# A layernorm, S4 convolution and gated MLP on one core: the last four token tiles' convolution sums in two halves, and a new order of instructions

## The chip, the cores and the metric

The kernel runs on one core of a Trainium2 chip. A core has five engines with queues of their own: TensorE (PE, matrix products), VectorE (DVE), ScalarE (ACT), GpSimd (POOL) and SyncE (SP). Here SP and POOL issue most DMA transfers. The metric is the device time of one execution in microseconds (us), as the median of several runs; lower is better.

## What is computed

The sum of three terms over 2048 tokens of 512 channels: the input x, an S4 layer's long convolution of the normalized input (its kernel is made from 128 complex modes per channel, and it has a skip term), and a gated MLP of the normalized input with 1792 hidden features.

```python
def reference(A_u, A_A_re, A_A_im, A_B_re, A_B_im, A_C_re, A_C_im, A_log_dt, A_Dskip, B_x, B_w_gate, B_w_up, B_w_down):
    def _A_ref(u, A_re, A_im, B_re, B_im, C_re, C_im, log_dt, Dskip):
        ...
        P = jnp.exp(logdA[:, :, None] * l[None, None, :])
        K = jnp.einsum("dn,dnl,dn->dl", Cc, P, dB).real
        ...
        Yf = Uf * Kf[None, :, :, :]
        ...
        y = (lambda x, *d: x.transpose(*d))(y, 0, 2, 1) + u * Dskip[None, None, :]
        return y
    def _B_ref(x, w_gate, w_up, w_down):
        g = jnp.einsum("bsd,df->bsf", x, w_gate)
        u = jnp.einsum("bsd,df->bsf", x, w_up)
        h = _sigmoid(g) * u
        return jnp.einsum("bsf,fd->bsd", h, w_down)
    x = A_u
    xn = _layernorm(x, axis=-1)
    return x + _A_ref(xn, A_A_re, A_A_im, A_B_re, A_B_im, A_C_re, A_C_im, A_log_dt, A_Dskip) + _B_ref(xn, B_w_gate, B_w_up, B_w_down)
```

Kf and Uf are Fourier transforms over 4096 points of the convolution kernel K and of the normalized input.

## The kernel before

Tokens are 16 tiles of 128 rows, `acc` holds the result and starts as x, `xn` the normalized input. Channels go in two halves of 256 (b = 0, 1). The work is cut into some 880 steps; a step is what one call of `add` records, and it issues one or several instructions on one engine. Names of steps used below, with the lines at which they are issued:

- norm0 to norm15 (L467 on DVE, L471 on ACT): layernorm of a tile. xT loads transpose it for the MLP.
- Kernel of the convolution, for each half b: parameters (around L635/L637), then levels Ha, Hc, Hd, He (L658 to L661), which build powers of 64 in `H`, and levels G1 to G16 (L694, L695, L698), which build the low powers in `G` through `tB`. All of these are DVE's. kgen (L723) multiplies both on PE into PSUM `pk`; ke (L338 on ACT, L339 on DVE, as all plain evictions from PSUM) copies it to `ks`; dump transfers write it to `kt_scr` in DRAM; exp transfers load it, spread, to `kf`.
- dsk (L779): one short DVE instruction that adds the skip term into row 0 of `kf`. It waits for the first two exp transfers of its half.
- s1k (L815): PE's first stage of the kernel's transform, `kf` to PSUM `pzk`; zke evicts, zkw writes to `zk_scr` in DRAM, lk loads it in another layout. The input goes the same way: s1x (L796), zse, zw, `z_scr`, lx.
- For eight groups of frequencies per half: px and pk (L935, 64x64 forms on PE) make the second stage, xe evicts px to a buffer in `H` or `xn`, two sw transfers copy it within the chip with its parts exchanged, kx copies pk to the ring (ACT), xk (L947, DVE) multiplies, or does so straight from PSUM, and kx falls away; pv (L963, PE) goes back one stage, ve evicts, vw writes to `v_scr`.
- inv (L989, PE): the last stage, for four token tiles (m = 0 to 3) in two inv steps each, from vp loads of `v_scr`; yo (L994, DVE) adds PSUM `py` to `acc`.
- The MLP in eight pairs of tiles: g and u steps (L834, eight matmuls each, called gate/up groups here), sig (L867, ACT), then up on ACT (L872) and a product of two ring buffers on DVE (L871), or the product straight from PSUM on DVE and no copy on ACT; d…a and d…b (L844, eight and six matmuls) are the down projection; ge (L889, DVE) adds it to `acc` for tiles 12 and up (`LATE` = 12), for the others ACT evicts, or DVE adds.
- sb and st transfers store `acc`: sb for tiles 0 to 11, st12 for tiles 12 and 13, st14 and st15.

The order of instructions on every engine is a written list: `ORDER` has the numbers of all steps, `OTHER` those which run on their other engine (DVE for ACT, POOL for SP), `SLOT` which of the ring, pair and PSUM buffers each use takes. Waits follow from these. Four PSUM buffers are shared by everything on PE, and 18 ring buffers (and more, from `tmp`, `G`, `gm` and `tB` when these are free) by the loads and evictions. A step carries a cost, a `move` time and, for a transfer, a `pre` time. `emit` reads none of the three:

```python
    def emit(self):
        for n in OTHER:
            t = self.tasks[n]
            t.eng, t.cost, t.fn = t.alt
        slots = dict(zip([b.n for b in self.bufs if b.kind in ROOM], SLOT))
        for n in ORDER:
            t = self.tasks[n]
            ...
            t.fn()
```

## Time and profile before

| | us |
| --- | --- |
| median of three runs | 229.45 |
| lowest and highest | 228.29, 232.39 |
| the profiled execution | 230.61 |
| its span | 228.8 |
| ACT busy in the span | 168.2 |
| POOL busy in the span | 74.1 |

The granted clock of TensorE was 0.996 in the profiled execution. The span goes from the first to the last instruction of the profile, and the execution's time has 1.81 us around it. All numbers of the trace are places or durations in that span. An arrow in a row (out<-in) tells what an instruction writes and reads; a row that joins several instructions has their number behind an x.

### The profile page before, as it was taken

How to read it: one execution, taken by the hardware profiler on the slowest of the kernel's cores; microseconds unless marked ns; L12 is line 12 of the kernel's file. 1: busy time of each engine (PE TensorE's matmuls, PEld its weight loads, DVE VectorE, ACT ScalarE, POOL GpSimd, SP SyncE). 2: the span in 40 equal slices, each digit the busy share in tenths (PEclk: the TensorE clock that was granted, in tenths of full speed). 3: DMA queues.
4: the chain of work that ended last, by engine and by line, in shares of the span. 5: the costliest groups of instructions: out<-in, count | busy, mean ns of one | idle time of the engine just before them, and what ended most of it. 6: DMA issues, size and time to landing. Idle time of an engine off the chain costs nothing.

```text
span 228.8 us, 5263 instructions
## 1 busy us (share of the span) xinstructions
PE 207.9 (91%) x2073; PEld 140.9 (62%) x2088; DVE 195.2 (85%) x262; ACT 168.2 (73%) x208; POOL 74.1 (32%) x122
## 2 busy tenths in 40 slices
PE   7698699999989999999897999999699979999691
PEld 2377586568774549887575644777567856556240
DVE  1899999999999999999999999984877869942782
ACT  2499999999899999999997608787697554761100
POOL 1105705100013350760251241369345514043220
PEclk9999999999999999999999999999999999999998
DMA  5997597260832545469744897568967896877854
GB/s 161 243 338 256 145 305 278 57 198 34 229 95 30 218 142 150 78 174 261 260 181 161 247 257 196 146 186 225 295 243 276 228 352 199 278 227 227 320 150 141
DMA packets 50121, 46.84 MB, mean 205 GB/s; under 512 B 16912, under 2 KB 41072, under 8 KB 50096
## 3 DMA queue, kind: packets, MB, share of 16 engines
q1 hardware_dynamic: 42000, 26.07, 40.9%
q0 software_dynamic: 6592, 19.12, 26.2%
q10 hardware_dynamic: 1504, 1.31, 2.2%
q8 instruction: 16, 0.26, 0.5%
q14 instruction: 9, 0.07, 0.1%
HBM read 24.82 MB, written 15.37 MB: 176 GB/s over the span
## 4 chain that ended last, share of the span: by engine, by line
PE 31%; DVE 31%; ACT 16%; DMA 12%; issue 6%; SPq 1%; POOL 1%; another core or an unknown queue 0%; ACTq 0%; POOLq 0%; DVEq 0%
PE pg L834 9%; DVE tB L694 6%; DVE G L695 6%; PE pu L834 6%; PE po L844 5%; DVE G L698 4%; DMA tmp<-zk_scr 4%; DVE ring L871 3%; DMA ring<-v_scr 3%; PE pv L963 2%; ACT ring L338 2%; PE pk L723 2%; DMA out_dram<-acc 2%; DMA kf<-kt_scr 2%; ACT ring L867 2%
## 5 line engine op out<-in xcount | busy, mean ns | idle before, releaser
L834 PEld LDWEIGHTS <-W 128*128 128x128 bf16 x896 | 85.2, 98 | 22.1 <-issue 9.6
L834 PE MATMUL pg<-ring,W 128*128 128x256 bf16 x512 | 62.1, 273 | 0.1
L834 PE MATMUL pu<-ring,W 128*128 128x256 bf16 x384 | 48.1, 273 | 2.7 <-DVE tmp L339 1.3
L844 PE MATMUL po<-wd,ring 128*128 128x512 bf16 x176 | 43.5, 379 | 0.7 <-issue 0.3
L844 PEld LDWEIGHTS <-ring 128*128 128x128 bf16 x184 | 17.3, 98 | 20.5 <-issue 2.4
L867 ACT ACTIVATE ring<-pg 128x1024 bf16<-128x1024 f32 (+1 forms) x27 | 24.3, 900 | 3.3 <-PE pg L834 3.1
L698 DVE TENSOR_TENSOR G<-G,tB 128x256 bf16<-128x256 bf16 (+4 forms) x20 | 19.7, 986 | 0.7
L694 DVE TENSOR_TENSOR tB<-G,gm 128x256 bf16<-128x256 bf16 (+4 forms) x20 | 19.6, 981 | 0.5
L872 ACT ACTIVATE ring<-pu 128x1024 bf16<-128x1024 f32 x14 | 14.3, 1028 | 7.3 <-PE pu L834 7.3
L695 DVE TENSOR_TENSOR G<-G,gm 128x256 bf16<-128x256 bf16 (+4 forms) x20 | 19.6, 979 | 0.0
L338 ACT ACTIVATE ring<-pzx 128x1024 bf16<-128x1024 f32 x16 | 16.2, 1037 | 0.8 <-PE pzx L796 0.7
L994 DVE TENSOR_TENSOR acc<-py,acc 128x1024 bf16<-128x1024 f32 x8 | 9.5, 1220 | 5.6 <-PE py L989 5.5
L435 DVE BATCH_NORM_STATS2 stats<-acc 128x6 f32<-128x512 bf16 x16 | 9.9, 679 | 4.6 <-DMA acc<-in_A_u_dram 4.6
L324 POOL DMA_DIRECT2D z_scr<-ring x9 | 5.0, 553 | 26.6 <-ACT ring L338 26.6
L723 PE MATMUL pk<-H,G 128*128 128x84 bf16 x256 | 10.5, 199 | 2.6 <-DVE G L698 2.0
L871 DVE TENSOR_TENSOR ring<-ring 128x1024 bf16<-128x1024 bf16 (+1 forms) x17 | 10.3, 606 | 2.7 <-ACT ring L872 2.7
L723 PEld LDWEIGHTS <-G 128*128 128x128 bf16 x256 | 9.9, 96 | 4.3 <-DVE G L698 3.3
L338 ACT ACTIVATE ring<-pzk 128x1024 bf16<-128x1024 f32 x11 | 11.0, 1036 | 1.7 <-PE pzk L815 1.2
L457 POOL TENSOR_TENSOR ve<-sd,half 128x2 bf16<-128x2 bf16 (+2 forms) x3 | 4.0, 1335 | 22.6 <-DVE sd L453 22.6
L324 POOL DMA_DIRECT2D kf<-kt_scr x18 | 10.2, 575 | 2.1 <-DMA kt_scr<-ks 1.7
L338 ACT ACTIVATE ks<-pk 128x1008 bf16<-128x1008 f32 (+1 forms) x10 | 9.0, 919 | 2.3 <-PE pk L723 2.2
L324 POOL DMA_DIRECT2D zk_scr<-ring x8 | 4.4, 548 | 17.3 <-ACT ring L338 17.3
(149 smaller groups left out, 373.4 us busy)
## 6 DMA issues: line engine op xcount, KB each, us to landing
z_scr<-ring POOLq DMA_DIRECT2D x9, 256.0 KB, 2.7
zk_scr<-ring POOLq DMA_DIRECT2D x8, 256.0 KB, 2.4
z_scr<-ring SPq DMA_DIRECT2D x7, 256.0 KB, 2.5
ring<-zk_scr SPq DMA_DIRECT2D x7, 256.0 KB, 4.1
v_scr<-ring POOLq DMA_DIRECT2D x7, 256.0 KB, 3.9
xn<-xn POOLq DMA_DIRECT2D x13, 128.0 KB, 3.7
ring<-z_scr POOLq DMA_DIRECT2D x6, 256.0 KB, 5.0
ring<-z_scr SPq DMA_DIRECT2D x5, 256.0 KB, 4.1
```

Source lines behind the costliest of these rows:

```text
L324: go = lambda e: lambda: q[e].dma_start(out=out(), in_=in_(), **(dict(transpose=True) if turn else dict(accum_op=ALU.add) if accum else {}))
L338: return self.p.add("ACT", 0.172 + n * 0.833e-3, lambda: nc.scalar.activation(out=dst(), in_=src(), func=ACT.Identity), after, rank, alt=( ...
L435: v.bn_stats(out=s["stats"][:, i, :], in_=self.acc[:, i, :])
L694: tt(out=t, in0=a, in1=m[1], op=ALU.mult)
L695: tt(out=o, in0=a, in1=m[0], op=ALU.mult)
L698: tt(out=z, in0=z, in1=x, op=ALU.add)
L723: nc.tensor.matmul(o, G[:, r, q].rearrange("p l c -> p (l c)"), H[:, r, :, CH * c + 4 * q:CH * c + 4 * q + 4], start=r == 0, stop=r == 1)
L834: nc.tensor.matmul(p[:, lo + n, :], W[:, i, kt, k * 128:(k + 1) * 128], xT(kt), start=kt == 0, stop=kt == KT - 1)
L844: nc.tensor.matmul(po[:, jj - base, :], hT[k // 4][:, k % 4, jj * 128:(jj + 1) * 128], wd[:, k, :], start=k == first, stop=k == FT - 1)
L867: e1 = add("ACT", 0.172 + n * 256 * 0.833e-3, lambda hT=hT, n=n, pg=pg: nc.scalar.activation(out=hT[:], in_=pg[:, 0:n, :], func=ACT.Sigmoi ...
L871: prod = lambda hT=hT, src=None: nc.vector.tensor_tensor(out=hT[:], in0=hT[:], in1=src(), op=ALU.mult)
L872: e2 = add("ACT", 0.172 + n * 256 * 0.833e-3, lambda ub=ub, pk=pk: nc.scalar.activation(out=ub[:], in_=pk(), func=ACT.Identity), mu, rk + ...
```

## The change

Three things are changed. First, `dma()` has other multipliers for the `move` and `pre` times of each kind of transfer; these are figures of the planner that wrote the lists, and no instruction depends on them. Second, for the last four token tiles (m = 3) the sum `yo` is made in two halves of two tiles each: each half waits for its own inv step alone, and stores of tiles 12 and 13 wait for the first half, those of 14 and 15 for the second. `conv_out[b, m]` becomes a list for that. Third, `ORDER`, `OTHER` and `SLOT` are new lists.

```diff
-        k, t.pre = dict(c1d=(1.22, 1.3), c3d=(1.22, 1.3), dump=(0.9, 1.15), exp=(1.3, 1.3), ld=(1.35, 1.2), lk=(1.16, 1.3), lx=(1.15, 1.7),
+        k, t.pre = dict(c1d=(1.15, 1.0), c3d=(1.15, 1.0), dump=(0.72, 1.25), exp=(1.3, 1.3), ld=(1.15, 2.4), lk=(1.25, 1.5), lx=(1.0, 1.9),
...
-            o = lambda m=m: acc[:, 4 * m:4 * m + 4, ND * b:ND * b + ND]
-            self.conv_out[b, m] = add("DVE", 1.22, lambda py=py, o=o: nc.vector.tensor_tensor(out=o(), in0=py[:], in1=o(), op=ALU.add),
-                                      ms + self.norm[4 * m:4 * m + 4] + [self.glu_out[i] for i in range(4 * m, 4 * m + 4) if i < LATE],
-                                      rk + m, use=[py], name=f"yo{b}{m}")
+            cuts = ((0, 4),) if m < LATE // 4 else ((0, 2), (2, 4))
+            self.conv_out[b, m] = []
+            for lo, hi in cuts:
+                o = lambda lo=lo, hi=hi, m=m: acc[:, 4 * m + lo:4 * m + hi, ND * b:ND * b + ND]
+                self.conv_out[b, m].append(add("DVE", 0.155 + (hi - lo) * ND * 1.042e-3, lambda py=py, lo=lo, hi=hi, o=o: nc.vector.tensor_tensor(
+                    out=o(), in0=py[:, lo:hi], in1=o(), op=ALU.add), ms[lo // 2:hi // 2] + self.norm[4 * m + lo:4 * m + hi] +
+                    [self.glu_out[i] for i in range(4 * m + lo, 4 * m + hi) if i < LATE], rk + m, use=[py], name=f"yo{b}{m}{lo or ''}"))
...
-                put(f"sb{b}{m}", 4 * m, 4, ND * b, ND * b + ND, done(4 * m, 4) + [self.conv_out[b, m]], 2 * m + b)
+                put(f"sb{b}{m}", 4 * m, 4, ND * b, ND * b + ND, done(4 * m, 4) + self.conv_out[b, m], 2 * m + b)
         for lo, n in ((12, 2), (14, 1), (15, 1)):
-            put(f"st{lo}", lo, n, 0, D, done(lo, n) + [self.conv_out[b, 3] for b in range(NBLK)], lo)
+            put(f"st{lo}", lo, n, 0, D, done(lo, n) + [self.conv_out[b, 3][lo > 13] for b in range(NBLK)], lo)
...
-    0, 1, 30, 2, 3, 31, 4, 5, 6, 7, 89, 8, 32, 9, 39, 10, 38, 90, 11, 12, 40, 33, 13, 91, 41, 42, 44, 92, 14, 43, 95,
+    0, 1, 30, 2, 3, 31, 4, 5, 6, 7, 89, 32, 8, 9, 38, 10, 90, 39, 11, 33, 12, 40, 91, 41, 13, 92, 37, 42, 44, 95, 43,
...
```

The instructions are the same apart from their places, but for a few that change engine. PE has the same 2089 matmuls, DVE 265 instructions for 264, ACT 223 for 220. By the lists: evictions of pv on DVE 8 to 3 and on ACT 8 to 13, of px 4 to 7 and 12 to 9, of pzk 2 to 4 and 14 to 12; one norm (norm3) from DVE to ACT; direct MLP products of 512 columns from PSUM 3 to 1; direct products of the spectra from PSUM 1 to 2. Loads of `zk_scr` on POOL: 2 to 5 of eight in the first half of the channels, 3 to 5 in the second; swaps on POOL 21 to 17, on SP 11 to 15; stores on POOL 5 to 2. In PE's order the array's form (128x128, 64x64 and so on) changes 70 times where it changed 78 times, 34 for 40 of them behind the last kgen.

What the lists do to the order is shown at three places. On DVE, between the parameters of the second half of the channels and its levels; `L779` is dsk0, of the first half. Before:

```order
L637 TENSOR_TENSOR H<-tmp 128x2x256
L637 TENSOR_TENSOR gm<-tmp 128x2x256
L658 TENSOR_TENSOR tB<-H 128x1024
L659 TENSOR_TENSOR H<-H 128x2x2x256
L660 TENSOR_TENSOR H<-H,tB 128x2x256
L661 TENSOR_TENSOR H<-H,tB 128x2x256
L694 TENSOR_TENSOR tB<-G,gm 128x256
L695 TENSOR_TENSOR G<-G,gm 128x64x4
L698 TENSOR_TENSOR G<-G,tB 128x64x4
L658 TENSOR_TENSOR tB<-H 128x3072
L659 TENSOR_TENSOR H<-H 128x2x1536
L660 TENSOR_TENSOR H<-H,tB 128x1536
```

and now:

```order
L637 TENSOR_TENSOR H<-tmp 128x2x256
L637 TENSOR_TENSOR gm<-tmp 128x2x256
L779 TENSOR_TENSOR kf<-kf,dsk 1x256
L658 TENSOR_TENSOR tB<-H 128x1024
L659 TENSOR_TENSOR H<-H 128x2x2x256
L660 TENSOR_TENSOR H<-H,tB 128x2x256
L661 TENSOR_TENSOR H<-H,tB 128x2x256
L694 TENSOR_TENSOR tB<-G,gm 128x256
```

dsk0 stood behind the wide levels (L658 to L661 with 1536 columns) and the first G level, and stands ahead of the narrow ones now.

On SP, the loads of `kf` for the second half of the channels; `H<-H` and `xn<-xn` are the swaps sw. Before:

```order
L324 DMA v_scr_66<-ring 128x4x256
L324 DMA kf<-kt_scr_69 16x4x256
L324 DMA kf<-kt_scr_69 32x3x256
L324 DMA kf<-kt_scr_69 16x2x256
L324 DMA H<-H 64x1024 x2
L324 DMA kf<-kt_scr_69 64x5x256
L324 DMA kf<-kt_scr_69 16x3x256
L324 DMA kf<-kt_scr_69 16x4x256
L324 DMA kf<-kt_scr_69 32x3x256
L324 DMA kf<-kt_scr_69 16x2x256 x2
L324 DMA kf<-kt_scr_69 16x4x256
L324 DMA kf<-kt_scr_69 32x2x256
```

and now:

```order
L324 DMA v_scr_66<-G 128x4x256
L324 DMA H<-H 64x1024
L324 DMA xn<-xn 64x1024
L324 DMA kf<-kt_scr_69 16x4x256
L324 DMA xn<-xn 64x1024
L324 DMA kf<-kt_scr_69 32x3x256
L324 DMA kf<-kt_scr_69 16x2x256
L324 DMA kf<-kt_scr_69 32x3x256
L324 DMA kf<-kt_scr_69 64x5x256
L324 DMA kf<-kt_scr_69 16x4x256
L324 DMA kf<-kt_scr_69 16x2x256
L324 DMA kf<-kt_scr_69 16x3x256
```

Swaps that stood in the middle of the loads stand ahead of them or behind the first.

On POOL, the loads of `zk_scr` for the second half of the channels (`ring<-` and `tmp<-zk_scr_65`). Before:

```order
L324 DMA v_scr_66<-ring 128x4x256
L324 DMA ring<-zk_scr_65 128x4x256 x2
L324 DMA H<-H 64x1024
L324 DMA xn<-xn 64x1024
L324 DMA H<-H 64x1024
L324 DMA ring<-zk_scr_65 128x4x256
L324 DMA H<-H 64x1024
L324 DMA tmp<-v_scr_66 128x1024
```

and now:

```order
L324 DMA H<-H 64x1024
L324 DMA ring<-zk_scr_65 128x4x256
L324 DMA tmp<-zk_scr_65 128x4x256
L324 DMA v_scr_66<-ring 128x4x256
L324 DMA ring<-zk_scr_65 128x4x256
L324 DMA H<-H 64x1024
L324 DMA ring<-zk_scr_65 128x4x256
L324 DMA v_scr_66<-ring 128x4x256
L324 DMA tmp<-zk_scr_65 128x4x256
```

Two more of these loads are POOL's, with writes of `v_scr` between them.

More of the change, by code (lines that the diff above doesn't have):

```diff
@@ L328, in dma @@
         kind = t.name[:2] if t.name.startswith("ld") else t.name.rstrip("0123456789_")
-        k, t.pre = dict(c1d=(1.22, 1.3), c3d=(1.22, 1.3), dump=(0.9, 1.15), exp=(1.3, 1.3), ld=(1.35, 1.2), lk=(1.16, 1.3), lx=(1.15, 1.7),
-                        sb=(1.0, 1.16), st=(1.15, 0.95), sw=(1.15, 1.2), vp=(1.3, 1.9), vw=(1.07, 1.4), xT=(0.3, 1.55), xa=(2.0, 2.1),
-                        zkw=(1.2, 0.8), zw=(0.95, 1.3))[kind]
+        k, t.pre = dict(c1d=(1.15, 1.0), c3d=(1.15, 1.0), dump=(0.72, 1.25), exp=(1.3, 1.3), ld=(1.15, 2.4), lk=(1.25, 1.5), lx=(1.0, 1.9),
+                        sb=(0.85, 1.55), st=(0.95, 1.1), sw=(1.25, 0.75), vp=(1.32, 2.0), vw=(0.95, 1.6), xT=(1.3, 0.75),
+                        zkw=(1.0, 0.95), zw=(1.1, 0.75))[kind]
         t.move *= k
```

110 rows, old and new, of tables (ORDER, OTHER, SLOT) are left out of this document.

## The prediction

> **What bounds the kernel now.** I read first the busy times, then DVE's busy tenths, the chain that ended last, and TensorE's (PE's) timeline for the places where it stood idle. Busy times, and DVE over the span in 40 slices of 5.7 us:
>
> ```profile
> PE 207.9 (91%) x2073; PEld 140.9 (62%) x2088; DVE 195.2 (85%) x262; ACT 168.2 (73%) x208; POOL 74.1 (32%) x122
> DVE  1899999999999999999999999984877869942782
> ```
>
> PE is busy for 207.9 of 228.8 us, and DVE is full from slice 3 to slice 25, so until about 143 us DVE sets the end, and afterwards it has room. The chain (start, duration, what) tells what took over:
>
> ```profile
> 141.40 2.30 DVE G L698
> 143.75 2.58 PE pk L723 x64
> ...
> 153.75 1.03 ACT H L338
> ...
> 158.00 4.54 DMA kf<-kt_scr
> ...
> 176.88 8.82 DMA tmp<-zk_scr
> ...
> 199.71 1.95 PE pv L963 x64
> ...
> 210.98 6.49 DMA ring<-v_scr
> ...
> 224.12 0.69 DVE acc L889
> ```
>
> The last step of DVE's levels (L698) ends at 143.70, the last kernel generation follows on PE, and from there transfers carry the chain: kf, zk and v loads. PE's waits in those stretches (start, duration, in brackets the idle time before and its end):
>
> ```profile
> 125.86 2.59 PE L723 MATMUL pk<-H,G 128*128 128x84 bf16 x64 [1.34 <-DVE G L698]
> 162.78 0.38 PE L815 MATMUL pzk<-kf,cst 128*128 128x512 bf16 x1 [1.74 <-DMA kf<-kt_scr]
> 185.74 0.41 PE L935 MATMUL pkf<-tmp 64*64 64x256 bf16 x8 [0.39 <-DMA tmp<-zk_scr]
> 188.67 1.91 PE L834 MATMUL pu<-ring,W 128*128 128x256 bf16 x16 [1.31 <-DVE tmp L339]
> 217.52 1.05 PE L989 MATMUL py<-ring,cst 128*64 128x512 bf16 x8 [2.30 <-DMA ring<-v_scr]
> ```
>
> So 5.7 us of PE waiting lie behind 143.70, and all but the product at 188.67 end with a transfer. No PE work is added or taken out, so the change can win these waits, PE's changes of form, and DVE time ahead of 143.70; nothing else reaches the end.
>
> **A. DVE up to its last level step.** The next rows are two groups of products and one of norms on DVE, the norm on ACT (instructions | busy, mean ns | idle), two DVE instructions, POOL's kf loads, and two rows of kf loads on POOL, early window and whole run (KB, us from issue to landing):
>
> ```profile
> L871 DVE TENSOR_TENSOR ring<-ring 128x512 bf16<-128x512 bf16 x5 | 2.1, 417 | 0.0
> L871 DVE TENSOR_TENSOR ring<-ring,pg 128x512 bf16<-128x512 bf16 x3 | 2.1, 686 | 0.3
> L467 DVE TENSOR_SCALAR xn<-acc,m_f,rinv 128x512 bf16<-128x512 bf16 x4 | 1.5, 408 | 0.0
> L471 ACT ACTIVATE xn<-acc,nb,rinv 128x512 bf16<-128x512 bf16 x12 | 9.4, 828 | 0.0
> 97.57 0.69 DVE L658 TENSOR_TENSOR tB<-H 128x1024 bf16<-128x1024 bf16 x1
> 105.82 0.27 DVE L779 TENSOR_TENSOR kf<-kf,dsk 1x256 bf16<-1x256 bf16 x1
> 95.36 5.07 POOL L324 DMA_DIRECT2D kf<-kt_scr  x9 [1.68 <-DMA kt_scr<-ks]
> kf<-kt_scr POOLq DMA_DIRECT2D x1, 32.0 KB, 2.8
> kf<-kt_scr POOLq DMA_DIRECT2D x3, 32.0 KB, 3.9
> ```
>
> norm3 goes to ACT: DVE loses 0.41 us, ACT gains 0.83 early, where it is behind nothing on the path. Of the direct products with pg one in this stretch becomes a product of two ring buffers: −0.69 + 0.42 us (ACT copies PSUM for it). Together −0.7. But dsk0 (L779) now stands ahead of the level step L658. DVE reaches that place at 97.57 less the gains up to there, some 97.3. dsk0 waits for the first two kf loads; exp01 is now second of POOL's kf issues, which begin at 95.36 and take 5.07/9 = 0.56 each, so it is issued at about 95.9 and lands 2.8 to 3.9 later, at 98.7 to 99.8. DVE then waits 1.4 to 2.5 us; the lower bound is 0.3, if POOL's row of issues, which waited 1.68 for a dump (row 95.36), starts a microsecond earlier. I take 1.4, by the row of the early window, which is this very stretch. In this kernel the same instruction at 105.82 found its loads long landed. Behind it on DVE wait all levels of the second half and thereby kgen on PE; no DVE idle time is left to hide it. A: +0.7 (−0.4 to +1.8).
>
> **B. The wait of 1.74 for kf.** SP's rows around the second half's loads:
>
> ```profile
> 154.84 1.24 SPq L324 DMA_DIRECT2D H<-H  x2
> 156.12 4.52 SPq L324 DMA_DIRECT2D kf<-kt_scr  x8
> ```
>
> Two swaps stand among SP's kf issues and wait for the eviction at 153.75 on ACT, which ends at 154.78; then eight kf issues follow, 0.56 each, and the last lands at 162.54. In the new order the swaps stand ahead of all but one of the kf issues and wait for evictions whose px come earlier on PE, by my count about 152.3, so the loads start some 2 us earlier. PE also has two more gate/up groups ahead of the first s1k (13 against 11, 0.86 us each by the rows under C). Both gains exceed 1.74. Its bounds are −1.74 and nothing (a transfer that lands no earlier since the DMA engines are full); I take −1.5. What is late next is the swap's own px, which waits for nothing new. The kf issues are moved past swaps of xn on SP, 0.6 each, and three kf issues stand behind swaps on POOL, which is idle there.
>
> **C. Changes of form on PE.** A px of form 64*64 between gate/up groups:
>
> ```profile
> 152.09 1.05 PE L834 MATMUL pu<-ring,W 128*128 128x256 bf16 x8
> 153.07 0.41 PE L935 MATMUL px<-ring,tmp 64*64 64x256 bf16 x8
> 153.31 0.39 PE L935 MATMUL px<-tmp 64*64 64x256 bf16 x8
> 153.63 2.79 PE L834 MATMUL pu<-ring,W 128*128 128x256 bf16 x24
> 205.30 1.89 PE L844 MATMUL po<-wd,ring 128*128 128x512 bf16 x8
> 207.02 1.91 PE L834 MATMUL pu<-ring,W 128*128 128x256 bf16 x16
> ```
>
> Start to start, the first px costs 0.24 and the second, which returns to 128*128, 0.32: 0.08 more for the way back; the group ahead takes 0.98 start to start, against 0.86 for eight matmuls (1.91 for 16 less 1.05 for 8), 0.12 for the way there. A round trip costs 0.2, or 0.32 where all that the second px took counts. By the order the number of changes falls from 78 to 70, 40 to 34 of them behind the last kgen: three round trips, −0.6 to −1.0; I take −0.8 between the two, with −0.6 and −1.3 (four trips) as bounds. Those ahead of 143.70 are covered by the wait of 1.34.
>
> **D. The zk loads.** Landings by queue, 256 KB each:
>
> ```profile
> ring<-zk_scr SPq DMA_DIRECT2D x7, 256.0 KB, 4.1
> ring<-zk_scr POOLq DMA_DIRECT2D x4, 256.0 KB, 6.3
> 180.00:190.00 10.00, 8.30 (x119) 6.65 (x118) 7.39 (x7) 5.50 (x6) 1.81 (x3) 1.00 0.97 293
> ```
>
> With B the zk writes end some 2.4 us earlier, and the loads behind them start so. Two more loads of the second half and three of the first go from SP to POOL, where a row has 2.2 us more to landing. POOL is busy 1.8 of 10 us at that time, so that queue is no stall. Of the gain of 2.4, 0.2 is left for such a load, the others keep it: PE's wait of 0.39 goes, −0.4 (bounds −0.4 and 0: the last row, the stretch 180 to 190, has the DMA engines busy to 0.97, at 293 GB/s).
>
> **E. The wait of 1.31.** A gate/up group waits for its PSUM buffer, freed by DVE's eviction of pv (L339). On DVE that stood behind the longest product:
>
> ```profile
> L947 DVE TENSOR_TENSOR H<-H,pkf 128x2048 bf16<-128x2048 bf16 x1 | 2.3, 2276 | 0.0
> ```
>
> In the new order there are two such products, but the pv evictions next to them are ACT's (8 to 13 on ACT). I take −0.8, nearer to the full 1.31 than to nothing, since one direct product more stays ahead of an eviction there (bounds −1.31 and 0).
>
> **F. s1k04 of the first half** comes three groups earlier, near 102.6, while its last kf load, eleventh on SP, is issued near 100 and lands at 103 to 104: PE waits 0.4 to 1.6, inside the 1.34 that it waits for DVE anyway at 125.86. 0 (0 to +0.7).
>
> **G. The tail.** Last pv, its eviction, write and first v load:
>
> ```profile
> 203.05 1.05 ACT L338 ACTIVATE tB<-pv 128x1024 bf16<-128x1024 f32 x1
> 204.12 0.36 SPq L324 DMA_DIRECT2D v_scr<-tB  x1
> 209.52 0.34 SPq L324 DMA_DIRECT2D tB<-v_scr  x1
> ```
>
> The last pv ends at 201.66, its eviction starts 1.39 later since ACT has three in a row. Now one of them is DVE's: the last write goes up to 1.4 earlier. But d15a, eight down matmuls, 1.72 us start to start (row C, 205.30 to 207.02), moves from ahead of the set of inv1 to behind it, so PE has that much less to do while it waits (2.30 now). Ends: −1.4 and +1.9; I take +0.4, by the difference of the two. SP's output stores stand behind the v loads and are no one's wait until the end.
>
> **H. The halves.** Two sums of 128x1024 become four of 128x512:
>
> ```profile
> L994 DVE TENSOR_TENSOR acc<-py,acc 128x1024 bf16<-128x1024 f32 x8 | 9.5, 1220 | 5.6 <-PE py L989 5.5
> ```
>
> By that row's slope and the last chain row (0.69 for 128x512), 4 × 0.69 − 2 × 1.22 = +0.3 us of DVE. It is idle 5.5 us there ahead of these sums, and the end is the down matmul and its sum at 224.12, not these: 0. A half may start one inv earlier (0.2 us), which the end doesn't see.
>
> **Sum.** 0.7 − 1.5 − 0.8 − 0.4 − 0.8 + 0.4 = −2.4. The profiled execution took 230.61 (span 228.8 and 1.8 around it), 1.16 above the median of 229.45; on it the sum gives 228.2, on the median 227.05, which I round to **227.0**.
>
> **Rivals.** *No gain:* the transfers are the bound; 0.97 at 180 to 190 speaks for it, 2 us earlier issues against it. B, D and E give nothing: 0.7 − 0.8 + 0.4 = +0.3, 229.75. *Larger gain:* every wait behind 143.70 goes and the tail's cover holds: A −0.4, B −1.7, C −1.3, D −0.4, E −1.3, G −1.4 = −6.5, 222.9; against it stands that they end with transfers of three kinds, each with its own queue and landing, and that all of these would have to come in time. *Slower, DVE's wait at dsk0:* the sum without that wait is −3.8 and each us of waiting goes into it. It decides from 3.8 us, that is, when exp01 lands later than 101.1, 5.2 after its issue. The two rows of such loads have 2.8 and 3.9; a load on POOL can take 6.3 (zk), which gives a wait of 4.9 and 230.6. *POOL's issues held up by DVE:* six issues of zk in a row, each held for half of a DVE product of 2.28, 1.1 us, make the last load 6.8 late; less the 2.4 of B that is +4.4, and with D gone 231.9. Against it speak nine kf issues at 0.56 each while DVE is full. The Trainium skill's page "SBUF — State Buffer", section "🔬 SBUF: two separate sides", says that a POOL-issued transfer can be kept from writing its descriptors while DVE copies, 620 ns alone becoming 3100; by that figure as an estimate, six issues would be 15 us late and the time near 240. POOL's row of 0.56 per issue does not agree with it.
>
> **Chances.** Forecast 0.45 (its own range 225.2 to 228.8), no gain 0.28, larger gain 0.14, dsk0 0.08, POOL 0.05. Low end 223.5 keeps most of the larger gain, high end 230.3 the no-gain case and the bounds of F and A. About 2% is what a measurement of this kernel can tell from no change: faster (under 224.9) takes nearly all of the larger gain and a little of the forecast, 0.18; slower (over 234) 0.04 from the last two, the rest 0.78.
>
> **What would show it.** A: DVE's idle time ahead of L779; none means A is −0.7, over 3.8 the slower rival. B: PE's wait ahead of the first pzk of the second half under 0.5 (1.74 now), and SP's kf issues in one row. C: 64*64 forms fewer, PE's busy time shorter. D, E: no waits for zk or L339 over 0.5. G: the wait ahead of the last py sets, 2.3 ± 1.5. Wrong it would be if kf landed no earlier, or the last level step ended after 145.

## The result and the profile after

| | before | changed |
| --- | --- | --- |
| median, us | 230.92 (4 runs, 228.29 to 232.86) | 237.81 (4 runs, 236.94 to 244.14) |
| profiled execution, span | 230.61, 228.8 | 238.50, 236.7 |
| mean granted clock in it | 0.996 | 0.977 |

The ratio is 1.0378, with a 95% interval of 1.027 to 1.0486: slower by 6.9 us in the medians, where 227.0 was forecast. Some executions of every kernel are slower than its others: medians here and below are of all executions, ratios and their intervals (always against the kernel before) leave the slow ones out, and where a profiled execution was far off, as in two of the experiments (424 and 720 us), the first trace is read up to 50 us only and the second not at all.

From the page of the changed kernel, busy times, DVE's busy tenths and the granted clock in tenths, in 40 slices of 5.9 us:

```profile
PE 212.9 (90%) x2074; PEld 143.6 (61%) x2088; DVE 195.4 (83%) x263; ACT 169.3 (72%) x210; POOL 74.3 (31%) x121
DVE  2899289999999999989999689988978668928283
PEclk9999589999999999999999999999999999999799
```

DVE is no longer full from 20 us on: counted from 0, it has a gap in slices 4 and 5 (24 to 36 us) and another in slice 22 (130 to 136 us). The clock is low in slices 4 and 5 and again near the end. The chain that ended last (start, duration, what):

```profile
13.67 11.70 DMA W<-in_B_w_up_dram
25.41 1.89 PE pu L834 x8
...
105.64 3.87 DMA kf<-kt_scr
...
131.54 3.04 DMA zk_scr<-ring
...
136.88 4.12 DMA ring<-zk_scr
...
152.28 2.41 PE pk L723 x64
...
209.02 5.58 DMA v_scr<-tmp
...
217.30 5.07 DMA tmp<-v_scr
```

Before, the chain ran on DVE up to 143.70. Now transfers are in it from 13.67 us on: the weights of the up projection, kf and zk of the first half of the channels. The last generation of the kernel starts at 152.1 instead of 143.75. PE's waits:

```profile
25.41 1.89 PE L834 MATMUL pu<-ring,W 128*128 128x256 bf16 x8 [3.27 <-DMA W<-in_B_w_up_dram]
109.65 0.38 PE L815 MATMUL pzk<-kf,cst 128*128 128x512 bf16 x1 [1.56 <-DMA kf<-kt_scr]
131.30 1.91 PE L834 MATMUL pg<-ring,W 128*128 128x256 bf16 x16 [1.75 <-ACT ring L338]
172.20 1.46 PE L815 MATMUL pzk<-kf,cst 128*128 128x512 bf16 x5 [0.55 <-DVE xn L339]
194.05 0.41 PE L935 MATMUL pkf<-ring,tmp 64*64 64x256 bf16 x8 [0.70 <-DMA ring<-zk_scr]
222.42 0.64 PE L989 MATMUL py<-tmp,cst 128*64 128x512 bf16 x2 [3.46 <-DMA tmp<-v_scr]
```

Behind the last generation two waits fell about as forecast, 1.74 to 0.55 and 1.31 to nothing; the one for zk rose, 0.39 to 0.70, and that of the tail too, 2.30 to 3.46. Ahead of it three waits are new, 6.6 us together; the kernel before has one of 1.69 at 25.61 in their place. What DVE made of them, the first level step (L658) and the third set's second half (L694 after L871) of the kernel before first:

```profile
36.73 0.69 DVE L658 TENSOR_TENSOR tB<-H 128x1024 bf16<-128x1024 bf16 x1 [0.28 <-ACT H L604]
...
129.06 0.29 DVE L694 TENSOR_TENSOR tB<-G,gm 128x256 bf16<-128x256 bf16 x1
```

and the changed kernel:

```profile
30.75 1.22 DVE L871 TENSOR_TENSOR ring<-ring,pu 128x1024 bf16<-128x1024 bf16 x1 [5.41 <-PE pu L834]
...
41.71 0.68 DVE L658 TENSOR_TENSOR tB<-H 128x1024 bf16<-128x1024 bf16 x1
...
102.40 0.27 DVE L779 TENSOR_TENSOR kf<-kf,dsk 1x256 bf16<-1x256 bf16 x1
102.60 0.67 DVE L658 TENSOR_TENSOR tB<-H 128x1024 bf16<-128x1024 bf16 x1
...
128.42 2.29 DVE L698 TENSOR_TENSOR G<-G,tB 128x4096 bf16<-128x4096 bf16 x1
...
137.00 0.29 DVE L694 TENSOR_TENSOR tB<-G,gm 128x256 bf16<-128x256 bf16 x1 [1.40 <-ACT G L684]
```

So 5.0 us are lost by 41.71, after DVE has waited 5.41 us for PE; the same lateness stands at 102.60 (5.0 behind 97.57), and at 137.00 it is 7.9. From there to the last chain row before (224.12) and its counterpart 8.5 us later (232.57) it changes little: 2.5 us are won behind the last generation and lost in the tail.

Steps are named by numbers in the text below. In u0_8, 0 is the pair of tiles and 8 the first of the step's blocks of hidden features. In kgen100, the third generation, 1 and 0 are the second half of the channels and its first set; kgen110 to kgen1124 are the last generation. kgen100 needs DVE's step G16_10, three instructions with 4096 columns of which the L698 that ends at 130.71 is the last; DVE's next level, G1_11 (the L694 at 137.00), comes behind kgen100. p50 and s20 are parameter steps on DVE and ACT.

### The profile page after: what moved, and what is told of

Read it like the earlier page. It is cut to its first block, busy times and chain, and to the rows that moved or that the text cites. A ratio compares the mean times of both kernels' runs of the same rounds, so it can differ in the third digit from the quotient of the medians.

```text
span 236.7 us, 5282 instructions
## 1 busy us (share of the span) xinstructions
PE 212.9 (90%) x2074; PEld 143.6 (61%) x2088; DVE 195.4 (83%) x263; ACT 169.3 (72%) x210; POOL 74.3 (31%) x121
## 3 DMA queue, kind: packets, MB, share of 16 engines
q10 hardware_dynamic: 1776, 1.44, 2.3%
## 4 chain that ended last, share of the span: by engine, by line
PE 25%; DVE 23%; DMA 19%; issue 14%; ACT 7%; SPq 6%; POOL 4%; POOLq 0%; DVEq 0%
PE pg L834 7%; PE po L844 7%; SPq L324 6%; DMA W<-in_B_w_up_dram 5%; DVE tB L694 4%; PE pu L834 4%; DMA ring<-zk_scr 4%; DVE G L698 4%; DVE G L695 4%; DMA kf<-kt_scr 3%; DMA v_scr<-tmp 2%; DMA tmp<-v_scr 2%; DVE ring L871 2%; PE pzk L815 2%; ACT ring L338 2%
## 5 line engine op out<-in xcount | busy, mean ns | idle before, releaser
L834 PE MATMUL pg<-ring,W 128*128 128x256 bf16 x512 | 64.0, 276 | 2.8 <-ACT ring L338 1.8
L844 PE MATMUL po<-wd,ring 128*128 128x512 bf16 x153 | 37.6, 379 | 0.4
L867 ACT ACTIVATE ring<-pg 128x1024 bf16<-128x1024 f32 (+1 forms) x23 | 21.2, 928 | 7.8 <-PE pg L834 6.1
L844 PEld LDWEIGHTS <-ring 128*128 128x128 bf16 x160 | 15.2, 98 | 18.3 <-issue 1.5
L694 DVE TENSOR_TENSOR tB<-G,gm 128x256 bf16<-128x256 bf16 (+4 forms) x20 | 19.6, 981 | 1.9 <-ACT G L684 1.4
L698 DVE TENSOR_TENSOR G<-G,tB 128x256 bf16<-128x256 bf16 (+4 forms) x20 | 19.7, 985 | 0.7
L871 DVE TENSOR_TENSOR ring<-ring,pu 128x1024 bf16<-128x1024 bf16 x6 | 7.3, 1219 | 8.4 <-PE pu L834 8.4
L997 DVE TENSOR_TENSOR acc<-py,acc 128x1024 bf16<-128x1024 f32 (+1 forms) x10 | 9.5, 1003 | 5.1 <-PE py L989 5.1
L949 ACT ACTIVATE ring<-pkf 128x1024 bf16<-128x1024 f32 x9 | 9.0, 1022 | 6.5 <-PE pkf L935 6.5
L844 PE MATMUL po<-wd,tmp 128*128 128x512 bf16 x44 | 11.5, 379 | 0.0
L413 PE MATMUL zp<-ks 128*128 128x512 bf16 x29 | 9.7, 501 | 1.4 <-POOL ks L402 1.4
L338 ACT ACTIVATE ring<-pzk 128x1024 bf16<-128x1024 f32 x7 | 7.2, 1033 | 5.2 <-DMA zk_scr<-ring 2.8
```

Of the source, the lines that this page charges most:

```text
L338: return self.p.add("ACT", 0.172 + n * 0.833e-3, lambda: nc.scalar.activation(out=dst(), in_=src(), func=ACT.Identity), after, rank, alt=( ...
L694: tt(out=t, in0=a, in1=m[1], op=ALU.mult)
L698: tt(out=z, in0=z, in1=x, op=ALU.add)
L834: nc.tensor.matmul(p[:, lo + n, :], W[:, i, kt, k * 128:(k + 1) * 128], xT(kt), start=kt == 0, stop=kt == KT - 1)
L844: nc.tensor.matmul(po[:, jj - base, :], hT[k // 4][:, k % 4, jj * 128:(jj + 1) * 128], wd[:, k, :], start=k == first, stop=k == FT - 1)
L867: e1 = add("ACT", 0.172 + n * 256 * 0.833e-3, lambda hT=hT, n=n, pg=pg: nc.scalar.activation(out=hT[:], in_=pg[:, 0:n, :], func=ACT.Sigmoi ...
```

## Experiments on the first 35 us

PE's wait of 3.27 us: u0_8 needs the last load of the up weights (768 KB). In the DMA views of the kernel before and of the changed one it lands 9.3 and 11.7 us after its issue:

```profile
W<-in_B_w_up_dram SPq DMA_DIRECT2D x1, 768.0 KB, 9.3
```

```profile
W<-in_B_w_up_dram SPq DMA_DIRECT2D x1, 768.0 KB, 11.7
```

The new order issues three loads of tokens 8 to 15 (256 KB each) between its issue and its landing, and puts u0_8 and u0_12 ahead of three steps that wait for nothing. In the nine profiles with these loads early that are read here it lands 9.7 to 12.4 us after its issue, in the nine with them late 8.4 to 10.0.

**Tokens early, old order.** In the kernel before:

```diff
 SP:   ... ld_w11024
+      ld_x80
       xT3
-      ld_x80
 POOL: hold1
+      ld_x81 ld_x121
       ... c1d00
-      ld_x81 ld_x121
```

> Kernel before, but with the loads of tokens 8 to 15 issued early as in the changed kernel. Theory (late landing of W_up alone costs nothing when u0_8 stands at 26.7): W_up lands near 25.3, PE's wait at u0_8 under 0.3, time within 1 us of the kernel before. Rival (these loads cost time in themselves): 2 us or more above the kernel before.

229.78 against 228.83 us, ratio 1.0016 (0.9969 to 1.0062). The up weights landed after 11.2 us and PE did not wait for them. The early loads alone cost nothing.

**Up steps later, new order.**

```diff
 PE:
-g0_12 u0_4 u0_8 u0_12 u0_6 g0_8 g0_10 u0_10
+g0_12 u0_4 u0_6 g0_8 g0_10 u0_8 u0_12 u0_10
```

> Changed kernel, but on PE u0_6, g0_8 and g0_10 stand ahead of u0_8 and u0_12 again. Theory (u0_8 waits for the last load of W_up while three groups behind it wait for nothing, and DVE's product waits for u0_6 with all levels behind it): no wait over 1 us at u0_8, no low granted clock at 25 to 31, the first level step on DVE at 37 to 38.5 instead of 41.9, time 4 to 5 us below the changed kernel, 232.5 to 234. Rival (the clock fell for a reason of its own): clock low at 24 to 31 again and the first level step after 40, time as the changed kernel, 237 to 238.

239.27 us, ratio 1.0378 (1.0277 to 1.0478): nothing won. The wait for the weights is down to 0.80, but PE then waits for a PSUM buffer that ACT frees, since sig0_12 keeps its early place on ACT, and DVE's p50 waits for s20 behind it. The first level step came at 39.5. In PE's timeline:

```profile
31.66 4.23 PE L834 MATMUL pg<-ring,W 128*128 128x256 bf16 x24 [2.78 <-ACT ring L867]
```

**Tokens later, new order.** ld_x80 behind xT3, ld_x81 and ld_x121 behind c1d10.

> Changed kernel, but the loads of tokens 8 to 15 (x80, x81, x121) are issued behind the transposing load xT3 and c1d10, as before the change. Theory (these loads take DMA time from the load of W_up, which lands 2.2 us later for it): W_up lands 9.3 us after its issue instead of 11.7, PE's wait at u0_8 falls from 3.3 to about 1.0, clock stays up, first level step at 37.5 to 39, time 233 to 235. Rival (the place of u0_8 alone makes the wait): the wait stays at 2.5 or more, time 236.5 to 238.

244.82 us, ratio 1.0668 (1.0561 to 1.0776): worse. The first half of the theory held, the weights landed after 8.4 us and PE had no wait at u0_8. But the new order has also put DVE's statistics of these tokens ahead of p50 and the levels, and they wait for the tokens; the first level step came at 42.4. In DVE's timeline:

```profile
34.70 1.88 DVE L435 BATCH_NORM_STATS2 stats<-acc 128x6 f32<-128x512 bf16 x3 [6.04 <-DMA acc<-in_A_u_dram]
```

**All of it mended, new order, with d15a as cover** (below).

```diff
 PE:  u0_6 g0_8 g0_10 ahead of u0_8
 ACT:
-norm7 sig0_12 up0_12 c110 c100 c1n0 norm2 ... s20 zse2 c20 g000
+norm7 c110 c100 c1n0 sig0_12 up0_12 s20 g000 norm2 ... zse2 c20
 DVE: p50 behind pr0_4
```

> Changed kernel with d15a as cover, and with the first 35 us mended: u0_6, g0_8, g0_10 ahead of u0_8 on PE; on ACT the evictions c110, c100, c1n0 ahead of sig0_12, and s20 and g000 right behind up0_12; on DVE p50 behind pr0_4. Theory (the early stall is worth 1.6 to 5 us at the first level step, but PE's waits from 90 to 131 hold kgen100 back in any case): first level step at 36.5 to 38, kgen100 at 129 to 131, time 232 to 234. Rival (the early stall is the whole loss): kgen100 at 126 to 127, time 229 to 230. Other rival (PE alone sets kgen100, the early stall of DVE costs nothing): kgen100 at 131 to 133, time 235 to 236 as the run with d15a alone.

237.60 us, ratio 1.0308 (1.0227 to 1.039), 2.4 us above the run with d15a alone by the medians; the intervals overlap. The wait moved once more (3.32 us at 32.88, for ACT), the first level step was at 39.7 and kgen100 at 131.9. None of the three forecasts held, and the trace can't weigh the early part: its clock was already down to 0.85 from 10 to 20 us, ahead of the steps that were moved. This early order is a knot of PE, ACT and DVE in which each mended wait returned elsewhere.

## Experiments between 90 and 155 us: which engine is late

**Less PE work.** 48 matmuls of group 1 are left out (the products over the last three quarters of the channels in eight gate/up steps), in both orders, so that PE has some 5 us less to do between 98 and 125 us:

```diff
-                for kt in range(KT):
+                for kt in range(nk):
...
-[...] mms(p, lo + h, i, (k + h, k + h + 1), xT),
+[...] mms(p, lo + h, i, (k + h, k + h + 1), xT, 1 if g == 1 and k in (4, 8) else KT),
```

> Kernel before, with three quarters of the matmuls of eight gate/up steps of group 1 left out (the products over the last three quarters of the channels; 48 matmuls, about 5.2 us of PE, all between 98 and 113 us). Theory (in this order DVE's levels set the start of kgen100 and PE has room): PE's wait ahead of kgen100 grows from 1.34 to 5 us or more, kgen100 stays at 125.9 within 0.4, time within 1 us of the kernel before. Rival (PE sets the pace here too): kgen100 3 us or more earlier.

230.12 against 229.93 us, ratio 1.0014 (0.9964 to 1.0065). kgen100 stayed where it was (125.86 before), right behind DVE's last step:

```profile
125.94 2.59 PE L723 MATMUL pk<-H,G 128*128 128x84 bf16 x64 [2.08 <-DVE G L698]
```

The wait ahead of it grew to 2.1 only; the rest of the room showed as small waits on the way. In the old order DVE sets the pace there, and less work on PE wins nothing. How much later PE may come without loss, this doesn't show: the kernel before has the wait of 1.34 and no more.

> Changed kernel, with the same matmuls left out. Theory (in the new order PE's waits have made PE late, so that PE and not DVE sets the start of kgen100): kgen100 follows the end of G16_10 within 0.4 us instead of 2.2 to 4.2, G1_11 starts at most 11.8 us behind the start of G16_10 instead of 13.1, time 2 to 4 us below the changed kernel. Rival (waits for buffers and transfers, not PE's amount of work, hold kgen100): kgen100 still 1.5 us or more behind G16_10, time as the changed kernel.

235.09 us, ratio 1.0201 (1.0124 to 1.0278), 2.7 below the changed kernel by the medians; the intervals just touch.

> Changed kernel with d15a as cover and with the same 48 matmuls of group 1 left out as in the two runs before (in the run of the changed kernel without d15a the one profiled execution was disturbed, 720 us, and its trace can't be read). Theory (PE is late in the new order): kgen100 at most 1 us behind the end of G16_10 instead of 4.2 in the run with d15a alone, time 231.5 to 233.5. Rival (waits for buffers hold it): kgen100 2.5 us or more behind G16_10, time 234.5 to 236.

234.32 us, ratio 1.0234 (1.0123 to 1.0345), against 235.18 with d15a alone. In the run with d15a alone, DVE's L698 and kgen100:

```profile
125.00 2.29 DVE L698 TENSOR_TENSOR G<-G,tB 128x4096 bf16<-128x4096 bf16 x1
```

```profile
131.58 2.62 PE L723 MATMUL pk<-H,G 128*128 128x84 bf16 x60
```

PE starts kgen100 4.3 us behind DVE's step (it ends at 127.29), though DVE was only 1.5 us behind its place in the kernel before. With less PE work:

```profile
106.23 0.59 PE L815 MATMUL pzk<-kf,cst 128*128 128x512 bf16 x2 [2.75 <-DMA kf<-kt_scr]
...
129.29 1.98 PE L723 MATMUL pk<-H,G 128*128 128x84 bf16 x48
133.07 0.76 PE L723 MATMUL pk<-H,G 128*128 128x84 bf16 x16 [1.80 <-ACT ring L867]
```

Of 5.2 us less work, 2.1 reached the start of kgen100 (2.2 behind L698's end at 127.05, where it was 4.3), since the wait for kf took back 0.6 and waits for ACT more, and its last part then waited for ACT: half the theory, half the rival. At the end 1.0 us of it is left in the two traces, and between the two ratios no difference clear of their intervals. With less work PE comes earlier, but its waits hold it.

**s1k04 two steps later, new order** (behind g1_0; zke04 behind sig1_8, zkw04 ahead of sw02_1 on POOL).

> Changed kernel, but s1k04 of the first half stands two gate/up groups later on PE (behind g1_0), its eviction and write behind sig1_8. Theory (PE, not DVE, sets the start of kgen100 at 133.1, so its wait of 1.6 to 2.1 us for kf passes to the end): the wait for kf under 0.4, kgen100 1 to 2 us earlier against the first level step than in the changed kernel (91.2 us after it there), time 235 to 237. Rival (DVE's levels set the start): kgen100 stays at 91 us behind the first level step, time 237 to 239.

239.66 us, ratio 1.0318 (1.021 to 1.0425): nothing won. The wait for kf fell to 0.57, and the next one, which the constants' load behind the kf loads on SP ends, was 2.10:

```profile
109.37 0.59 PE L815 MATMUL pzk<-kf,cst 128*128 128x512 bf16 x2 [0.57 <-DMA kf<-kt_scr]
...
112.06 0.63 PE L935 MATMUL px<-ring,tmp 64*64 64x256 bf16 x16 [2.10 <-DMA tmp<-c_w]
```

**kgen100 ahead of the waiting pair, new order.** g6_0, g6_2 and sig6_0 behind kgen1024 and its eviction.

> Changed kernel, but the group pair g6_0, g6_2 (and its sigmoid on ACT) stand behind kgen1024 and its eviction, so kgen100 doesn't stand behind g6_0's wait of 1.75 us for a PSUM buffer. Theory (PE is late for kgen100 by 2.2 us behind DVE's last step G16_10): kgen100 starts within 0.5 us of the end of G16_10, DVE's next level G1_11 1 to 2.5 us earlier against G16_10, time 235 to 236.5. Rival (the waits only move behind kgen): G1_11 as late as before, 13.1 us behind the start of G16_10, time 237 to 239.

241.20 us, ratio 1.0438 (1.0329 to 1.0548). kgen100 still came 1.9 us behind the end of G16_10 (127.85; 2.3 in the changed kernel), since it now waited for a PSUM buffer itself:

```profile
129.78 2.67 PE L723 MATMUL pk<-H,G 128*128 128x84 bf16 x64 [1.11 <-ACT ring L872]
```

G1_11 was 1 us nearer to the start of G16_10, as the theory says; then the pair that was moved made PE 2 us late for kgen110.

**Another ring buffer, new order with d15a as cover.** PE's wait of 1.75 at 131.30 ends with ACT, and ACT waits for a write: zke00 and sig6_0 take ring buffer 1 in turn, each when the write from it has landed. In ACT's timeline of the changed kernel:

```profile
130.22 1.02 ACT L338 ACTIVATE ring<-pzk 128x1024 bf16<-128x1024 f32 x1 [2.79 <-DMA zk_scr<-ring]
...
134.68 1.02 ACT L867 ACTIVATE ring<-pg 128x1024 bf16<-128x1024 f32 x1 [1.60 <-DMA zk_scr<-ring]
```

```diff
-zke00: ring buffer 1      up5_8: ring buffer 10      zkw06 on SP
+zke00: ring buffer 10     up5_8: ring buffer 1       zkw06 on POOL
```

On DVE the product pr5_8 changes places with pr5_0 for it.

> Changed kernel with d15a as cover; zke00 takes ring buffer 10 instead of 1 (1 was held by the write zkw06 that had to land first), up5_8 takes 1, and zkw06 is issued by POOL instead of SP. Theory (the writes' landing by way of one ring buffer makes PE late ahead of kgen100): ACT's zke00 starts 0.5 to 1 us earlier, kgen100 at most 3.3 us behind the end of G16_10 instead of 4.2, G1_11 0.7 to 2 us earlier against G16_10 than the 14.4 of the run with d15a alone, time 233.5 to 234.8. Rival (only PE's total of work and waits counts): G1_11 within 0.4 of the run with d15a alone, time as that run, 235 to 236.

240.04 us, ratio 1.0422 (1.0289 to 1.0554): nothing won. The wait was this one: kgen100 stood 2.1 us behind G16_10 instead of 4.2, and G1_11 12.0 us behind the start of G16_10 instead of 14.4. But PE's next wait, for zk, grew from 1.37 to 2.82, and the last generation was 1.5 us later than in the run with d15a alone (the first level step 1.1 us): PE was late for kgen110 instead.

```profile
130.35 2.58 PE L723 MATMUL pk<-H,G 128*128 128x84 bf16 x64
...
139.64 0.64 PE L935 MATMUL pkf<-ring,tmp 64*64 64x256 bf16 x8 [2.82 <-DMA ring<-zk_scr]
```

## Experiments behind the last generation

**Old order up to kgen1124, new order behind it**, without and with d15a as cover (19 ring buffers chosen anew where the two overlap).

> Order of the kernel before up to the last kernel generation kgen1124, then the order of the changed kernel, halves included (some ring buffers chosen anew where the two overlap). Theory (all of the loss lies ahead of kgen1124 and in the tail, the stretch between gains 2.6 us and the tail loses as much): kgen1124 at 145 to 146.5, end of the last pv 2 to 3 us earlier than in the kernel before, wait ahead of inv10 3 us or more, time within 1.5 us of the kernel before. Rival (the stretch behind kgen1124 gains only because everything came late): last pv not earlier, time 2 us or more above the kernel before.

> As the run with the old order up to kgen1124, but d15a ahead of inv10 to inv16 as cover. Theory: 2 to 3 us below that run, that is 226 to 227.5 and 1 to 2.5 us below the kernel before. Rival: the wait moves to the next inv, time as the run without it.

233.43 us, ratio 1.0133 (1.0044 to 1.0222), and 230.80 us, ratio 1.0063 (1.0015 to 1.0111). With d15a, the last generation starts at 144.15 (143.75 before) and the last pv at 201.39 (201.03 before): nothing is won between the two. The rival of the first run held. PE's waits there:

```profile
165.52 1.46 PE L815 MATMUL pzk<-kf,cst 128*128 128x512 bf16 x6 [1.11 <-DMA kf<-kt_scr]
170.41 0.59 PE L815 MATMUL pzk<-kf,cst 128*128 128x512 bf16 x2 [0.82 <-ACT G L338]
188.12 0.41 PE L935 MATMUL pkf<-ring,tmp 64*64 64x256 bf16 x8 [0.49 <-DMA ring<-zk_scr]
198.53 0.63 PE L963 MATMUL pv<-H,tmp 64*64 64x256 bf16 x16 [0.62 <-DVE xn L947]
```

With one of 0.56 at 147.29 they are 3.6 us, against 3.4 in the kernel before and 1.3 in the changed one: on time, the same order waits again. That the late start alone made the changed kernel's waits small is not shown. In the other executions with this order and a late start (149.4 to 152.2) they vary from 1.1 to 3.9 us, and the 19 other buffers may have a part. The two runs show more plainly where the time goes: with d15a as cover in both, the new order throughout takes 235.18 us (ratio 1.0156 to 1.0335), and with the old order up to kgen1124 230.80.

**The kf wait alone, old order.** SP's swaps sw05_1 and sw06_1 behind the last kf load; then also dsk1 ahead of xk05 on DVE.

> Kernel before, but SP's two swaps sw05_1 and sw06_1 are issued behind SP's last kf loads of the second half instead of in their middle (DVE's product xk05, which needs one of them, stays in its place on DVE). Theory of the prediction (B): kf loads issued 1.2 us earlier, PE's wait of 1.74 falls to about 0.5, time 1 to 1.5 us below the kernel before. Rival (the loss of this wait is given back by the next transfers and by what waits for the swaps): wait shorter or moved to pv05, time within 0.5 us of the kernel before.

> As the run with the two swaps behind the kf loads, and dsk1 ahead of xk05 on DVE, so that s1k10 no longer stands behind a product that waits for the moved swap. Theory of the prediction (B): PE's wait at the first pzk of the second half 0.3 to 0.8 us instead of 1.74, the following waits no longer, time 0.7 to 1.5 us below the kernel before. Rival (what is won there is lost at the next transfers): the wait falls but waits behind it grow, time within 0.5 us of the kernel before.

233.17 us, ratio 1.0159 (1.0096 to 1.0223; of two executions only), and 233.15 us, ratio 1.0065 (1.0003 to 1.0127). In the first the wait is longer, since dsk1 stands on DVE behind the product that waits for the moved swap; in the second it is gone, and there is one at pv05 instead:

```profile
164.06 0.39 PE L815 MATMUL pzk<-kf,cst 128*128 128x512 bf16 x1 [3.12 <-DVE kf L779]
```

```profile
161.29 0.38 PE L815 MATMUL pzk<-kf,cst 128*128 128x512 bf16 x1 [0.20 <-ACT xn L338]
164.78 0.63 PE L963 MATMUL pv<-H,tmp 64*64 64x256 bf16 x16 [2.03 <-DVE ring L871]
```

The wait at pv05 is made by the edit itself: pv05 needs the product xk05, which needs the swap that was moved behind the loads; DVE waits 3.87 us for that swap now, 2.25 before. So the two runs don't show what the earlier loads are worth alone; the new order has these swaps ahead of the loads, and that was not tried in the old one. The second profiled execution took 229.43 us, 1.2 less than the kernel before in its own, but the comparison of the runs shows no gain, and the halves alone, with the old order, were 1.2 faster too between the last generation and the last pv (56.1 us; 57.3 before). Most executions of both kernels had a mean granted clock of 0.981 to 0.993, where most of the kernel before had 0.989 to 1.0; why is open.

**d15a as cover, new order; d15a late, old order.**

```diff
 PE, new order:
-inv04 inv10 inv12 inv06 inv14 inv16 d15a d15b
+inv04 d15a inv10 inv12 inv06 inv14 inv16 d15b
 PE, old order:
-inv08 inv010 d15a inv14 inv16 inv18 inv110 d15b
+inv08 inv010 inv14 inv16 inv18 inv110 d15a d15b
```

> Changed kernel, but d15a stands ahead of inv10 to inv16 on PE, as cover for the loads of v. Theory (the tail is 3 us longer because 1.7 us of work were moved behind the wait and the long wait lowers the clock): wait ahead of inv10 at most 1.8 instead of 3.46, no low clock behind it, last down matmul 2 to 3 us earlier, time 235 to 236. Rival (the v loads land later for the work moved and the wait only shifts): time as the changed kernel, 237 to 238.

> Kernel before, but with d15a behind inv14 to inv110 on PE, so that it no longer covers the wait for v. Theory: wait ahead of inv14 near 4.0 us instead of 2.3, last down matmul 1.5 to 3 us later, time 1.5 to 3 us above the kernel before. Rival (the wait was long enough for all): time as before.

235.18 us, ratio 1.0245 (1.0156 to 1.0335), 2.6 below the changed kernel by the medians, though the intervals overlap; and 233.79 us, ratio 1.0135 (1.0055 to 1.0215), 4.2 above the kernel before by the medians and 3.1 by the ratio. The first is as expected, the second a little more. The traces are clearer. From the start of the last pv to that of the last six matmuls, in the kernel before, the changed one and the changed one with d15a as cover:

```profile
201.03 0.63 PE L963 MATMUL pv<-H,tmp 64*64 64x256 bf16 x16
222.63 1.46 PE L844 MATMUL po<-wd,ring 128*128 128x512 bf16 x6
```

```profile
206.85 0.61 PE L963 MATMUL pv<-xn,tmp 64*64 64x256 bf16 x16
231.08 1.46 PE L844 MATMUL po<-wd,ring 128*128 128x512 bf16 x6
```

```profile
205.61 0.61 PE L963 MATMUL pv<-xn,tmp 64*64 64x256 bf16 x16
227.22 1.46 PE L844 MATMUL po<-wd,ring 128*128 128x512 bf16 x6
```

That is 21.6, 24.2 and 21.6 us: the cover takes back the whole loss of the tail. In the old order with d15a late the tail takes 25.8, and the wait in it 3.71 where it was 2.30.

**Halves alone, old order.**

> Order of the kernel before, with the sums of tiles 12 to 15 made in two halves and nothing else. Theory (0.3 us of DVE work off the path): time within 0.5 us of the kernel before. Rival (halves free PSUM later or delay the last sums): 1 us or more above.

230.26 against 229.61 us, ratio 1.0002 (0.9959 to 1.0046): nothing, as expected.

No version beat the kernel before.

## Why the prediction was wrong

The step that failed is in the reading, "the change can win these waits, PE's changes of form, and DVE time ahead of 143.70; nothing else reaches the end". It took PE's room ahead of the last generation for granted: F put a new wait of up to 1.6 us at nothing because it lay "inside the 1.34" that PE waits for DVE, and the stretch up to 40 us has no term in the sum at all. The runs showed a PE that comes late in both places. Starts in the traces, in us:

| | before | changed | changed, d15a as cover |
| --- | --- | --- | --- |
| DVE's first level step | 36.73 | 41.71 | 38.24 |
| end of G16_10 on DVE | 125.80 | 130.71 | 127.29 |
| kgen100 on PE | 125.86 | 133.04 | 131.58 |
| last generation on PE | 143.75 | 152.12 | 150.59 |
| last pv | 201.03 | 206.85 | 205.61 |
| last six matmuls | 222.63 | 231.08 | 227.22 |

DVE needs 89 us from the first row to the second in all three. PE has the same steps ahead of kgen100 in both lists, so it isn't late for more work. By its timelines it waits 8.6 us in all up to kgen100 before, 11.9 in the changed kernel and 13.2 with d15a as cover; the rest of the 7.2 and 5.7 us is time in which its matmuls ran slower. With the early loss down to 1.5 us, the last generation is still 6.8 late: the larger part of the loss is PE's on the way to it, and not the early stall. That the loss lies ahead of the last generation is shown by the run with the old order up to there, 230.80 against 235.18 us. Which of the waits makes how much of it stays open, since each one that was mended came back at the next. None of the prediction's rivals had this mechanism.

- **A** was wrong by its size, in a direction that doesn't matter: DVE had no wait at dsk0. L779 runs at 102.40, right behind the step before. SP's kf issues began at 100.21, with exp00 first; exp01, second of POOL's as the prediction says, was issued at about 101.4, and no kf load of that stretch landed in less than 1.7 us, so it cannot have been waited for. dsk0 writes only row 0 of the first token columns, which exp00 alone loads: the list's two loads order the plan, the wait follows the data. The −0.7 is not to be seen either: from the first L658 of the second half to the end of G16_10, 28.1 us now (102.60 to 130.71) and 28.2 before (97.57 to 125.80).
- **B, D, E**: B and E were about right on the waits in the changed kernel (1.74 to 0.55, 1.31 to none), D was wrong (0.39 to 0.70). Their worth hung on the execution. From the last generation to the last pv the pair of traces has 57.3 us before and 54.7 now; in five traces with the old order there it is 56.1 to 59.8, in seven with the new order and a late start 54.7 to 57.8, and in the two that start on time 57.0 and 57.2. So the 2.5 us of the one pair is no safe figure, and on time nothing is seen. The rival "no gain" is what these parts did.
- **C** is mostly not to be seen: without its waits, PE takes 53.7 us in that stretch before and 53.3 now, at most 0.4 of the −0.8.
- **F** had the wait (1.56; 0.4 to 1.6 was said) and the wrong cover. The 1.34 that PE waited for DVE was slack only if PE came there in time. The waits at 109.65, 125.89 (0.67) and 131.30 are 4.0 us together and passed it, with DVE itself 5.0 us late. In place of 0 to +0.7, kgen100 started 2.3 us behind DVE's step in the changed kernel and 4.3 with d15a as cover.
- **G** was mis-sized: +0.4 taken, −1.4 to +1.9 as range, +2.6 measured (21.6 and 24.2 us). The earlier write held in part: the v load that PE waits for ended 15.0 us behind the last pv instead of 15.9. But PE's work in this stretch is the same, and without d15a ahead of it the wait is 1.2 longer; the other 1.5 is mostly PE's work at a lower clock (0.78 from 219 to 225), for which the sum had no term.
- **H** held: the halves alone give 1.0002.
- The rival on POOL's issues: nothing in the runs speaks for it; POOL's zk loads in the changed kernel landed in 4.5 us (6.3 before).

The early loss itself differs between executions. The changed kernel and five of the experiments have the same order up to there:

| | wait for the weights at u0_8 | mean clock, 20 to 30 us | first level step |
| --- | --- | --- | --- |
| changed kernel | 3.27 | 0.72 | 41.71 |
| s1k04 two steps later | 2.84 | 1.00 | 40.67 |
| another ring buffer | 3.03 | 1.00 | 39.39 |
| kgen100 ahead of the pair | 2.40 | 1.00 | 38.81 |
| d15a as cover | none | 1.00 | 38.24 |
| less PE work, d15a as cover | 1.44 | 1.00 | 38.16 |
| kernel before | none | 1.00 | 36.73 |

So at the full clock this order loses 1.4 to 3.9 us, by when the weights land and by smaller waits ahead of them, and the changed kernel's 5.0 holds the low clock besides: five gate/up groups from 25.41 on took 7.2 us, where they take 4.4 in the run with d15a as cover. The early part was not mended as a whole in any run, so its worth at the end stays open.

## What to carry to other kernels

Of a replanned order, list the waits of every engine from the start, not only those on the present chain: an engine that has room keeps it only as long as nothing ahead of it takes it. A wait that ends with a transfer is not worth its length in a sum until an order with this change alone has shown it, and what gives way to the transfer can wait in its place, as the moved swap did here. Read a gain of 1 or 2 us from several traces: the same order took 56.1 to 59.8 us in one stretch. Work that covers a wait near the end is paid in full when it is moved behind it, and here the lower clock behind the longer wait was paid besides.

## What the runs showed of the hardware

PE's low clock follows waits, but the length of the wait alone doesn't decide it. In the changed kernel the groups behind the wait of 3.27 took 1.71 us where 0.87 is usual, at a mean clock of 0.72 from 20 to 30 us:

```profile
20.00:30.00 10.00, 6.51 (x38) 4.77 (x39) 5.27 (x11) 4.93 (x7) 0.35 (x1) 0.72 1.00 223
```

In the run with another ring buffer the wait at the same place was 3.03 us, and the clock behind it 1.00. In the run of the old order with d15a late, the same wait of 1.69 us at 25.6 that the kernel before has was followed by a clock of 0.8 in two slices, and the first level step was 1.7 us later than in the kernel before, where no such fall is seen. The clock row of its page:

```profile
PEclk9999889999999999999999999999999999999589
```

In the tail all five waits for v of 3.46 to 4.39 us were followed by pairs of inv matmuls that took 0.42 to 0.46 us each, where 0.22 to 0.25 is usual. Behind waits of 2.30 and 2.32 us they ran as usual, behind one of 2.20 us (the halves alone) at half that speed.

The Trainium skill's page "TensorE: Matmul & The Clock Gate", section "🔬 Part 1: The HAM clock gate (the "warmup" mystery)", says that the clock falls after an idle window of about 3.4 us and that the windows run free, so that runs differ. The five waits of 3.46 us and more agree with it; the falls behind waits of 1.69, 2.20 and 3.27 us stand behind waits shorter than the window it names.
